# Decode attention with gate and feed-forward: all output weights behind the last values, in runs of eight heads

## The chip, the cores and the metric

The kernel runs on one core of a Trainium2 chip. The core has five engines with instruction queues of their own: TensorE (PE, matrix products), VectorE (DVE), ScalarE (ACT), GpSimd (POOL) and SyncE (SP, which here only issues transfers). Sixteen DMA engines move data between HBM and the on-chip memory (SBUF). Engines wait for each other and for transfers on semaphores. The metric is the time of one execution on the device, in microseconds (us); lower is better. All data is float32.

## The reference

Two batch items, one new position each. The attention block has 32 heads of 128, with a cache of 4096 keys and values per head; the feed-forward block has 1728 hidden units. The result mixes both by a gate:

```python
g = sigmoid((x * gate_w).sum(-1, keepdims=True))          # x: (2, 1, 640)
q = (x @ wq).reshape(B, 1, 32, 128).transpose(0, 2, 1, 3)  # wq: (640, 4096)
p = softmax(einsum("bhqd,bhkd->bhqk", q, k_cache) * 128 ** -0.5)
o = einsum("bhqk,bhkd->bhqd", p, v_cache)                  # caches: (2, 32, 4096, 128)
a = o.transpose(0, 2, 1, 3).reshape(B, 1, 4096) @ wo       # wo: (4096, 640)
b = silu(x @ w1) @ w2                                      # w1: (640, 1728), w2: (1728, 640)
return g * a + (1 - g) * b
```

The caches are 134 MB each, the weights 10.5 MB (wq), 10.5 MB (wo) and 4.4 MB each (w1, w2).

## The kernel before

**Items.** Four heads of one batch item are an item: 16 items, each with 8.4 MB of keys and 8.4 MB of values. SBUF has three large buffers ("slabs") of 8.4 MB, a, b and v. Keys of even items go to b, of odd items to a; values go to v, but those of the last item (15) go to b, in three pieces. The layout is `p c`: partition p holds 128 positions of one head.

**One item.** `query(i)` spreads the item's queries over the partitions (TensorE). `products(i)` multiplies keys with the query in place: GpSimd 60 of the 128 positions of a partition, VectorE 68 (L617). `scores(i)` sums over the head dimension (VectorE, L627), `peak(i)` takes the maximum, `weights(i)` the exponential (ScalarE), which writes the tile `pz`. In the next turn `total`, `values` (32 products of width 512 on TensorE, L707, twice that in records of the profile), `invert`, `combine` (scale and pick out, VectorE), `gather` (TensorE) and `turn` finish the item. `turn` sums the four heads' columns into `row`, transposes it by 32 x 32 blocks and writes the item's columns of `oP`, a tile for each group of four heads with columns for both batch items (0 and 16).

**The order.** Each engine runs its operations in the order in which `f.op` and `f.dma` record them; `Flow.plan` derives the waits from what each reads and writes. All large transfers are issued by SP, in order; an issue waits until the buffer's readers are done, and everything recorded behind it on SP waits with it. In the loop over items SP gets values(i), then keys(i + 2). On TensorE, items 0 to 13 run as loops (one before and one after the middle), where waits are counted down on the semaphores `next_q`, `weights`, `values` and `rows`; the rest is straight code.

**Weights.** SP starts with wq into a and v, w1 into v and keys 0 into b; keys 1 follow when the first part of the query projection has freed a. x and the gate vector are issued by ScalarE. Around item 5 (`MID`), slab a takes the output weights of groups 0 and 1 and w2 in place of keys 7: `project(0)`, `project(1)` and `ffn_out` run there, then keys 7 are loaded. The output weights of groups 2 to 7 go into v after the values of item 14, as six transfers of 1280 KB, the last one cut in 960 and 320 KB.

**The end.** `project(grp)` multiplies a group's four columns with its weights. Groups 0 to 5 are "early": their sums go to two strips of a PSUM bank, width 320. Groups 6 and 7 are "late": four strips, width 160. After the first column of the late ones `merge` copies the early sums (ScalarE, L548) and joins them in (TensorE, L553). VectorE copies the result (L844), SP stores it, and when it has landed GpSimd clears the semaphores (L850).

Of the kernel before, what the change touches and what calls it, by code (L numbers as in the profile page):

```python
# [4 lines left out]
AF = mybir.ActivationFunctionType  # L5
# [137 lines left out]
def gated_decode(nc, x, kc, vc, wq, wo, w1, w2, gate, out):  # L143
    P = 128
# [39 lines left out]
    def part(n, *ks):  # L184
        return [f"{n}.{k}" for k in (ks or range(8))]
# [18 lines left out]
    he = sb("he", [P, FR, B])  # L204
    seq = sb("seq", [P, 2 * FR, B])
    join = sb("join", [P, 2, HB + 1])
    qall = sb("qall", [P, HQ, B, DH])
    qsb = sb("qsb", [P, DH])
    Ss = [sb(f"s{i}", [P, C]) for i in range(2)]
# [1 line left out]
    rs = sb("rs", [P, 1])  # L211
    rg = sb("rg", [P, 1])
    osb = sb("osb", [P, 4, DH])
    turned = sb("turned", [P, 512])
    spaced = sb("spaced", [P, FR, 32])
    row = sb("row", [P, DH])
    oP = [sb(f"oP{i}", [P, Q, 32]) for i in range(HQ)]
    oT = sb("oT", [P, Q, 32])
    partial = sb("partial", [P, W2])
    ot = sb("ot", [P, W])  # L220

# [8 lines left out]
    W1_AT = (J - J0) * H * DH  # L230
    XG_AT = W1_AT + J * F
    HD = D // 2
    WO_MID = 2
    WO_AT = {}
    for grp in range(HQ):
        WO_AT[grp] = FH * HD + grp * QD * D // P if grp < WO_MID else (grp - WO_MID) * QD * D // P
# [17 lines left out]
    def load_v(i):  # L254
        src = run_of(vflat, i)
        if i < N - 1:
            v_load[i] = f.dma("SP", slab["v"], src, writes=part("v"), signal=h_v if i < LOOPED else None)
            return
        cuts = (0, SLAB // 2, 3 * SLAB // 4, SLAB)
        after = f.users(part("b"))  # L260
        for k, (c0, c1) in enumerate(zip(cuts, cuts[1:])):
            f.dma("SP", slab["b"][:, c0:c1], src[:, c0:c1], writes=part("b", k), after=after)

    def load_wo(grp, n, key, after):
        at = WO_AT[grp]
        src = wo[grp * QD : (grp + 1) * QD, :].rearrange("(p n) d -> p (n d)", n=Q)
        cuts = (0, Q * D - D, Q * D) if grp == HQ - 1 else (0, Q * D)
        for k, (c0, c1) in enumerate(zip(cuts, cuts[1:])):
            f.dma("SP", slab[n][:, at + c0 : at + c1], src[:, c0:c1], writes=part(n, key + k), after=after)
# [6 lines left out]
    f.dma("ACT", xg[:B], x.rearrange("b s d -> (b s) d"), writes=part("v", 6))  # L276
    f.dma("ACT", xg[B : B + 1], gate[None, :], writes=part("v", 7))
    f.dma("SP", slab["v"][:, :W1_AT], wq_rows[:, SLAB:], writes=part("v", 0))
    f.dma(
        "SP",  # L280
# [14 lines left out]
    )  # L295
    f.op("POOL", lambda: G_.memset(xz, 0.0), writes=["xz"])
    f.op("POOL", lambda: G_.memset(pz, 0.0), writes=["pz"])
    f.op("POOL", lambda: G_.memset(partial, 0.0), writes=["partial", "partial2", "partial3"])
# [22 lines left out]
    f.op("DVE", lambda: V.memset(pick, 0.0), writes=["pick"])  # L321
    f.op(
        "DVE",
        lambda: V.reduce_sum(pick[:, 0:P:32], sel.rearrange("p (q c) -> p q c", c=4), axis=AX.X),
        reads=["sel"],
        writes=["pick"],
    )
# [2 lines left out]
        lambda: V.reduce_sum(own, sel.rearrange("p (q c) -> p c q", c=4), axis=AX.X),  # L330
        reads=["sel"],
        writes=["own"],
    )
    for q in range(Q):
        f.op(
# [177 lines left out]
    for e in range(2):  # L513
# [51 lines left out]
    def project(grp, n, key):  # L565
        w = slab[n][:, WO_AT[grp] : WO_AT[grp] + Q * D]
        to = "early" if grp < LAST else "late"
        for k in range(Q):
            lhsT = oP[grp][:, k, :] if count[to] == 0 else oP[grp][:, k, : HB + 1]
            wk = part(n, key + (grp == HQ - 1 and k == Q - 1))  # L570
            accumulate(lhsT, w[:, k * D : (k + 1) * D], [f"oP{grp}", f"oP{grp}b"], wk, to)
            if count["late"] == 1:
                merge()

    def ffn_out(n):

        def fn():  # L580
            for k in range(FH):
                to = 64 + 32 * (k % 2)
                last = T_.matmul(  # L583
                    early[to : to + 2 * B, :],
                    seq[:, k : k + 2, :].rearrange("p k b -> p (k b)"),
                    slab[n][:, k * HD : (k + 1) * HD],
                    start=(k < 2),
                    stop=(k >= FH - 2),
                )
            return last  # L590

        f.op("PE", fn, reads=["seq0", "seq1"] + part(n, 2), writes=["ps_acc"])
# [106 lines left out]
        )  # L699

    def values(i, by=(), loop=None):
        v = slab["v" if i < N - 1 else "b"].rearrange("p (g c) -> p g c", g=NG)

        def groups(g0, g1):
            for gr in range(g0, g1):
# [22 lines left out]
        for k, (g0, g1) in enumerate(zip(cuts, cuts[1:])):  # L728
            f.op(
                "PE",  # L730
                lambda g0=g0, g1=g1: groups(g0, g1),
                reads=part("b", k) + ["pz"],
                writes=["ps_v"],
            )

# [25 lines left out]
        )  # L761

    def turn(i):
        hq, b = items[i]
        f.op(
            "DVE",
            lambda: V.reduce_sum(row, ps_o.rearrange("p (c d) -> p d c", d=DH), axis=AX.X),  # L767
            reads=["ps_o"],
            writes=["row"],
        )  # L770
        dst, key = (oP[hq], f"oP{hq}") if b == 0 else (oT, "oT")
        f.op(
            "DVE",
            lambda: V.transpose(dst, row.rearrange("p (i n) -> p n i", n=Q)),
            reads=["row"],
            writes=[key],
        )
        if b == 1:
            f.op(
                "DVE",  # L780
                lambda: V.tensor_copy(oP[hq][:, :, HB : HB + 1], oT[:, :, 0:1]),
                reads=["oT", f"oP{hq}"],
                writes=[f"oP{hq}b"],
            )

    for i in range(N + 1):
# [12 lines left out]
        if i < N and i != MID:  # L801
            load_v(i)
        if i < N:
            scores(i)
            if 1 <= i <= LOOPED:
                relay(i)
            if i + 2 < N and i != MID:
                load_k(i + 2)
            peak(i)
            weights(i)  # L810
        if i == MID:
            after = f.users(part("a"))
            for grp in range(WO_MID):
                load_wo(grp, "a", grp, after)
            f.dma(
                "SP",
                slab["a"][:, : FH * HD],
                w2.rearrange("(p r) (e c) -> p (r e c)", p=P // 2, e=2).rearrange("p (e c) -> (p e) c", e=2),
                writes=part("a", 2),
                after=after,  # L820
            )
            load_v(i)
        if i == N - 1:
            after = f.users(part("v"))
            for grp in range(WO_MID, HQ):
                load_wo(grp, "v", grp - WO_MID, after)
# [4 lines left out]
        if i == 0:  # L831
            query(1)
        elif i + 1 < N:
            query(i + 1, by=by("relay"), loop=loop)
# [7 lines left out]
    for grp in range(WO_MID, HQ):  # L842
        project(grp, "v", grp - WO_MID)
    f.op("DVE", lambda: V.tensor_copy(ot, acc), reads=["ps_acc"], writes=["ot"])  # L844
    left = f.dma("SP", out.rearrange("b s (n d) -> (s n) b d", n=G), ot[0:P:HB, :], reads=["ot"])

    def clear():
        ids = sorted(s.num for s in f.sems)
        assert ids == list(range(ids[0], ids[-1] + 1))
        return G_.sem_clear(range(ids[0], ids[-1] + 1))  # L850

    f.op("POOL", clear, after=[left])

# [36 lines left out]
```

## Time and profile before

| | before |
|---|---|
| median of 3 runs | 697.12 us (696.89 to 698.07) |
| profiled execution | 697.13 us |
| its span | 695.1 us |
| HBM read | 298.26 MB, 429 GB/s over the span |
| busiest engine | VectorE, 479.2 us (69%) |
| TensorE | 223.0 us (32%) |

The span runs from the first to the last instruction; the execution's own time has 2.0 us more around it. PE is TensorE's products, PEld its weight loads, SPq and ACTq the issuing of transfers by SyncE and ScalarE. A float32 product stands in the profile as two records. In a timeline row the first number is the start, the second the length, and the bracket at the end the idle time before it and what ended it. The chain lists, in order of time, the work that each later step had to wait for, back from the last instruction.

### The profile page before, as it was taken

To read this page: it belongs to the slowest core of one execution; us is meant where nothing else is said; L and a number is where in the kernel's file an instruction comes from. 1 tells how busy PE (TensorE), PEld (TensorE's weight loads), DVE (VectorE), ACT (ScalarE), POOL (GpSimd) and SP (SyncE) were. 2 spreads that over 40 slices of the span, in tenths; PEclk is the share of its full clock that TensorE was granted. 3 is DMA by queue.
4 is the path that set the end of the run, shared out by engine and by line. 5 is a ranking of instruction groups with operands and counts; after the bars stand their busy time and mean duration, and the time that the engine had idled before them with its cause. 6 is when DMAs were issued, how large, how long until landed. Compare 5 with 4: busy or idle time off the path is not lost. (4 is left out here: it accounts for less than half of the span.)

```text
span 695.1 us, 3615 instructions
## 1 busy us (share of the span) xinstructions
PE 223.0 (32%) x1478; PEld 73.7 (11%) x1478; DVE 479.2 (69%) x236; ACT 40.8 (6%) x154; POOL 265.0 (38%) x25
## 2 busy tenths in 40 slices
PE   1630043240605053542140606041240605050376
PEld 1110011010201011110010202010010101010022
DVE  2016998969688695195949688694949588695930
ACT  0010001010101001001010101001010101001010
POOL 1006291808080624502609081533518080624400
PEclk9985556565757567877575757566575757566599
DMA  9999999999999999999999999999999999999997
GB/s 419 406 453 422 426 422 456 442 426 426 422 449 449 426 426 420 454 430 431 422 437 449 430 434 422 437 449 427 434 426 430 453 430 426 434 426 456 407 422 312
DMA packets 6794, 298.38 MB, mean 429 GB/s; under 512 B 759, under 2 KB 767, under 8 KB 1026
## 3 DMA queue, kind: packets, MB, share of 16 engines
q1 hardware_dynamic: 6780, 298.26, 99.3%
q8 instruction: 5, 0.08, 0.0%
q14 instruction: 3, 0.02, 0.0%
q10 hardware_dynamic: 6, 0.01, 0.0%
HBM read 298.26 MB, written 0.01 MB: 429 GB/s over the span
## 5 line engine op out<-in xcount | busy, mean ns | idle before, releaser
L707 PE MATMUL ps<-slab_v,pz 128*32 128x512 f32 x960 | 138.9, 743 | 352.9 <-PEq L129 326.8
L611 POOL TENSOR_TENSOR slab_b<-slab_b,qsb 128x7680 f32<-128x7680 f32 x8 | 131.4, 16428 | 203.9 <-DMA slab_b<-in_A_k_cache_dram 189.0
L611 POOL TENSOR_TENSOR slab_a<-slab_a,qsb 128x7680 f32<-128x7680 f32 x8 | 131.5, 16439 | 181.9 <-DMA slab_a<-in_A_k_cache_dram 168.5
L627 DVE TENSOR_REDUCE s<-slab_b 128x68 f32<-128x8704 f32 (+1 forms) x16 | 138.2, 8677 | 0.0
L627 DVE TENSOR_REDUCE s<-slab_a 128x68 f32<-128x8704 f32 (+1 forms) x16 | 138.1, 8676 | 0.0
L617 DVE TENSOR_TENSOR slab_b<-slab_b,ps 128x8704 f32<-128x8704 f32 x8 | 73.7, 9216 | 54.1 <-DMA slab_b<-in_A_k_cache_dram 54.1
L617 DVE TENSOR_TENSOR slab_a<-slab_a,ps 128x8704 f32<-128x8704 f32 x8 | 73.8, 9222 | 45.2 <-DMA slab_a<-in_A_k_cache_dram 42.8
L707 PEld LDWEIGHTS ps<-slab_v,pz 128*32 128x32 f32 x960 | 37.9, 133 | 441.5 <-issue 415.3
L656 ACT ACTIVATE pz<-s,nb 32x128 f32<-32x128 f32 x64 | 25.5, 398 | 547.4 <-PE ps L707 413.7
L755 PE MATMUL ps<-osb,pick 128*128 128x512 f32 x32 | 19.5, 694 | 26.8 <-PEq L129 24.9
L767 DVE TENSOR_REDUCE row<-ps 128x128 f32<-128x512 f32 x16 | 11.1, 692 | 22.3 <-PE ps L755 22.3
L739 DVE SCALAR_TENSOR_TENSOR osb<-ps,rg,own 128x512 f32<-128x512 f32 x16 | 12.0, 750 | 18.7 <-PE ps L707 18.7
L499 DVE COPY spaced<-ps 128x224 f32<-128x224 f32 x2 | 0.7, 387 | 27.8 <-PE ps L481 27.8
L432 PE MATMUL ps<-qall,spread 128*128 (+1 forms) x32 | 7.2, 310 | 25.4 <-DVE slab_b L617 24.7
L693 DVE RECIPROCAL ps<-ps 128x1 f32<-128x1 f32 x16 | 2.7, 169 | 16.9 <-PE ps L681 16.9
L535 PE MATMUL ps<-slab_v,oP 128*17 128x320 f32 (+2 forms) x128 | 11.9, 367 | 2.3 <-DMA slab_v<-in_A_wo_dram 2.2
L681 PE MATMUL ps<-rs,fold 128*128 128x1 f32 x32 | 6.1, 259 | 19.9 <-PEq L129 19.7
L412 PE MATMUL ps<-slab_a,xz 128*32 128x512 f32 x64 | 9.5, 758 | 8.6 <-DMA slab_a<-in_A_wq_dram 8.6
L656 ACT ACTIVATION_READ_ACCUMULATOR pz<-s,nb 32x1 f32 x64 | 11.8, 184 | 0.0
L583 PE MATMUL ps<-slab_a,seq 128*4 128x320 f32 x54 | 9.3, 501 | 7.5 <-DMA slab_a<-in_B_w_dram 7.5
L432 PEld LDWEIGHTS ps<-qall,spread 128*128 128x128 f32 x32 | 6.7, 216 | 34.9 <-DVE slab_b L617 25.5
L844 DVE COPY ot<-ps 128x160 f32<-128x160 f32 x1 | 0.3, 325 | 13.6 <-PE ps L535 13.6
(68 smaller groups left out, 97.4 us busy)
## 6 DMA issues: line engine op xcount, KB each, us to landing
slab_v<-in_A_wo_dram SPq DMA_DIRECT2D x5, 1280.0 KB, 18.2
slab_v<-in_B_w_dram SPq DMA_DIRECT2D x1, 4320.0 KB, 37.2
slab_a<-in_B_w_dram SPq DMA_DIRECT2D x1, 4320.0 KB, 27.5
slab_b<-in_A_v_cache_dram SPq DMA_DIRECT2D x1, 4096.0 KB, 37.9
slab_b<-in_A_v_cache_dram SPq DMA_DIRECT2D x2, 2048.0 KB, 44.5
slab_a<-in_A_wo_dram SPq DMA_DIRECT2D x2, 1280.0 KB, 16.2
slab_v<-in_A_wq_dram SPq DMA_DIRECT2D x1, 2048.0 KB, 26.3
slab_v<-in_A_wo_dram SPq DMA_DIRECT2D x1, 960.0 KB, 25.2
```

The lines of the kernel that those rows point to most:

```text
L412: last = T_.matmul(qr[u][32 * q : 32 * q + 32, :], xz[:, j, :], w[:, u * HALF : (u + 1) * HALF, q, :], start=(j == 0), stop=(j == J - 1),)
L432: return T_.matmul(ps_q[:, :DH], spread, qall.rearrange("p h b d -> p (h b) d")[:, i, :], start=True, stop=True,)
L535: last = T_.matmul(dst[32 * n : 32 * n + m, :], lhsT, w[:, n * width : (n + 1) * width], start=first, stop=final,)
L583: last = T_.matmul(early[to : to + 2 * B, :], seq[:, k : k + 2, :].rearrange("p k b -> p (k b)"), slab[n][:, k * HD : (k + 1) * HD], start ...
L611: lambda: G_.tensor_mul(k[:, CV:, :], k[:, CV:, :], qsb[:, None, :].to_broadcast([P, C - CV, DH])),
L617: lambda: V.tensor_mul(k[:, :CV, :], k[:, :CV, :], ps_q[:, None, :DH].to_broadcast([P, CV, DH])),
L627: lambda c0=c0, c1=c1: V.reduce_sum(Ss[i % 2][:, c0:c1], k[:, c0:c1, :], axis=AX.X),
L656: last = S_.activation(pz[lo:hi, :, 4 * q : 4 * q + 4], s[lo:hi].rearrange("p (g c) -> p g c", c=4), AF.Exp, bias=nb[lo:hi], scale=SCALE, ...
L707: last = T_.matmul(ps_v[32 * q : 32 * q + 32, :], pz[:, gr, :], v[:, gr, :], start=(gr < 4), stop=(gr >= NG - 4),)
L739: lambda: V.scalar_tensor_tensor(osb, ps_v.rearrange("p (c d) -> p c d", d=DH), rg, own[:, :, None].to_broadcast([P, 4, DH]), op0=ALU.mult ...
L755: lambda *_: T_.matmul(ps_o, pick, osb.rearrange("p c d -> p (c d)"), start=True, stop=True),
L767: lambda: V.reduce_sum(row, ps_o.rearrange("p (c d) -> p d c", d=DH), axis=AX.X),
```

## The change

- Output weights: none in the middle any more. All eight groups are loaded after the last values, in four runs of eight heads (2.6 MB each): runs 0 to 2 into v, run 3 into b in three pieces (1280, 960 and 320 KB). Runs 0 to 2 are early, run 3 is late. Each run is projected with eight columns.
- w2 is loaded in front, into b, ahead of the first keys, and `ffn_out` runs there. Keys of even items now go to a, of odd items to b; the first keys are issued where keys 1 were, values 0 after the first feed-forward product, keys 1 after `ffn_out`. The last values go to a.
- TensorE runs items 0 to 14 in one loop, with the query of the next item at its head.
- `turn` puts two groups into one tile: it sums on 64 partitions, copies the row twice side by side, transposes eight blocks instead of four and adds the two halves with masks (`side`), five or six VectorE operations instead of two or three.
- Ends: a first exponential on ScalarE, and the table load with it, stands ahead of the issues of x and the gate vector. The semaphores are cleared once SP has issued the output, and GpSimd waits for its landing after that; `s_out` and `s_sent` are counted down by their waits.

```diff
-    LAST = HQ - 2
+    NP = HQ // 2
+    PR = 2 * Q
...
-    MID = 5
-    LOOPED = N - 2
+    LOOPED = N - 1
+    s_out, s_sent = nc.alloc_semaphore("output"), nc.alloc_semaphore("sent")
...
     def kslab(i):
-        return "b" if i % 2 == 0 else "a"
+        return "a" if i % 2 == 0 else "b"
...
+    def load_wo(g):
+        n, at = ("v", g * PD) if g < NP - 1 else ("b", 0)
+        src = wo[g * PR * P : (g + 1) * PR * P, :].rearrange("(p n) d -> p (n d)", n=PR)
+        cuts = (0, PD) if g < NP - 1 else (0, PD // 2, PD - D, PD)
+        after = f.users(part(n)) if g in (0, NP - 1) else wo_after
         for k, (c0, c1) in enumerate(zip(cuts, cuts[1:])):
+            f.dma("SP", slab[n][:, at + c0 : at + c1], src[:, c0:c1], writes=part(n, g % (NP - 1) + k), after=after)
+        return after
...
-    load_k(0)
+    f.dma(
+        "SP",
+        slab["b"][:, : FH * HD],
+        w2.rearrange("(p r) (e c) -> p (r e c)", p=P // 2, e=2).rearrange("p (e c) -> (p e) c", e=2),
+        writes=part("b"),
+    )
...
+    f.op("ACT", lambda: S_.activation(ge, ones[:, :B], AF.Exp, scale=-1.0), reads=["ones"], writes=["ge"])
+    f.dma("ACT", xg[:B], x.rearrange("b s d -> (b s) d"), writes=part("v", 6))
+    f.dma("ACT", xg[B : B + 1], gate[None, :], writes=part("v", 7))
...
     f.op("PE", lambda: mm_qr(0, J0), reads=part("a") + ["xz"], writes=["ps_0", "ps_1"])
-    load_k(1)
+    load_k(0)
...
+    load_v(0)
...
-    total_of = {"early": Q * LAST, "late": Q * (HQ - LAST) + 1}
+    total_of = {"early": PR * (NP - 1), "late": PR + 1}
...
+    def project(g):
+        n, at = ("v", g * PD) if g < NP - 1 else ("b", 0)
+        w = slab[n][:, at : at + PD]
+        to = "early" if g < NP - 1 else "late"
+        for k in range(PR):
+            lhsT = oP[g][:, k, :] if count[to] == 0 else oP[g][:, k, : HB + 1]
+            key = g if g < NP - 1 else (k >= PR // 2) + (k == PR - 1)
+            accumulate(lhsT, w[:, k * D : (k + 1) * D], [f"oP{g}{u}{b}" for u in range(2) for b in range(B)], part(n, key), to)
             if count["late"] == 1:
                 merge()
...
+    ffn_out("b")
+    load_k(1)
...
     def turn(i):
         hq, b = items[i]
+        gr, u = divmod(hq, 2)
...
+        for e in range(2):
+            f.op("DVE", lambda e=e: V.tensor_copy(row2[:, :, 16 * e : 16 * e + 16], row.rearrange("p (i n) -> p n i", n=PR)), ...)
+        f.op("DVE", lambda: V.transpose(oT, row2), ...)
+        f.op("DVE", lambda: V.tensor_scalar(oE, oT[:, :, 0], side[:64, 0:1], None, op0=ALU.mult), ...)
+        f.op("DVE", lambda: V.scalar_tensor_tensor(oP[gr][64 * u : 64 * u + 64, :, HB * b], oT[:, :, 1], side[:64, 1:2], oE, op0=ALU.mult, op1=ALU.add), ...)
...
-            if 1 <= i <= LOOPED:
+            if i < LOOPED:
                 relay(i)
...
-        if i == MID:
-            after = f.users(part("a"))
-            for grp in range(WO_MID):
-                load_wo(grp, "a", grp, after)
-            f.dma("SP", slab["a"][:, : FH * HD], w2..., writes=part("a", 2), after=after)
-            load_v(i)
         if i == N - 1:
+            wo_after = None
+            for g_ in range(NP):
+                wo_after = load_wo(g_)
...
         if i + 1 < N:
+            query(i + 1, by=[ops["relay", i]], loop=i)
             copy_q(i + 1)
-        if i == MID:
-            for grp in range(WO_MID):
-                project(grp, "a", grp)
-            ffn_out("a")
-            load_k(i + 2)
+    for g_ in range(NP):
+        project(g_)
...
+    f.dma("SP", out.rearrange("b s (n d) -> (s n) b d", n=G), ot[0:P:HB, :], reads=["ot"], signal=s_out)
+    sent = f.op("SP", lambda: nc.sync.sem_inc(s_sent), after=[])
+    sent.signal = "sent"
     def clear():
         ids = sorted(s.num for s in f.sems)
+        G_.wait_ge(s_sent, 1).then_inc(s_sent, -1)
+        G_.sem_clear(range(ids[0], ids[-1] + 1))
+        return G_.wait_ge(s_out, 16).then_inc(s_out, -16)
```

More of the change, by code (lines that the diff above doesn't have):

```diff
@@ L206, in gated_decode @@
     join = sb("join", [P, 2, HB + 1])
+    turned = sb("turned", [P, FR * 32])
+    spaced = sb("spaced", [P, FR, 32])
+    oT, row2 = turned[:64, : PR * 32].rearrange("p (n r) -> p n r", r=32), spaced[:64, :PR, :]
     qall = sb("qall", [P, HQ, B, DH])
@@ L213, in gated_decode @@
     osb = sb("osb", [P, 4, DH])
[L214 to L218, printed above, removed]
+    row = sb("row", [64, DH])
+    oP = [sb(f"oP{i}", [P, PR, 32]) for i in range(NP)]
+    oE = sb("oE", [64, PR])
+    side = sb("side", [P, 2])
     partial = sb("partial", [P, W2])
@@ L232, in gated_decode @@
     HD = D // 2
[L233 to L236, printed above, removed]
+    PD = PR * D
     def kslab(i):
-        return "b" if i % 2 == 0 else "a"
+        return "a" if i % 2 == 0 else "b"
     kflat = kc.rearrange("b (g q) s d -> b g (q s d)", q=Q)
@@ L323, in gated_decode @@
         "DVE",
-        lambda: V.reduce_sum(pick[:, 0:P:32], sel.rearrange("p (q c) -> p q c", c=4), axis=AX.X),
+        lambda: V.reduce_sum(
+            pick.rearrange("p (a b) -> p a b", b=32)[:, : Q // 2, :2],
+            sel.rearrange("p (a b c) -> p a b c", b=2, c=4),
+            axis=AX.X,
+        ),
         reads=["sel"],
@@ L332, in gated_decode @@
         writes=["own"],
+    )
+    f.op(
+        "DVE",
+        lambda: V.reduce_sum(side, ident.rearrange("p (a e i) -> p e a i", e=2, i=16), axis=AX.XY),
+        reads=["ident"],
+        writes=["side"],
     )
@@ L563, in merge @@
         count["late"] += 1
[L565 to L571, printed above, removed]
+    def project(g):
[6 more added lines that the diff above has]
+            accumulate(lhsT, w[:, k * D : (k + 1) * D], [f"oP{g}{u}{b}" for u in range(2) for b in range(B)], part(n, key), to)
             if count["late"] == 1:
@@ L590, in fn @@
             return last
-        f.op("PE", fn, reads=["seq0", "seq1"] + part(n, 2), writes=["ps_acc"])
+        f.op("PE", fn, reads=["seq0", "seq1"] + part(n), writes=["ps_acc"])
         for k in range(2):
@@ L731, in values @@
                 lambda g0=g0, g1=g1: groups(g0, g1),
-                reads=part("b", k) + ["pz"],
+                reads=part("a", k) + ["pz"],
                 writes=["ps_v"],
@@ L764, in turn @@
         hq, b = items[i]
+        gr, u = divmod(hq, 2)
         f.op(
             "DVE",
-            lambda: V.reduce_sum(row, ps_o.rearrange("p (c d) -> p d c", d=DH), axis=AX.X),
+            lambda: V.reduce_sum(row, ps_o[:64].rearrange("p (c d) -> p d c", d=DH), axis=AX.X),
             reads=["ps_o"],
@@ L770, in turn @@
         )
-        dst, key = (oP[hq], f"oP{hq}") if b == 0 else (oT, "oT")
+        for e in range(2):
+            f.op(
+                "DVE",
+                lambda e=e: V.tensor_copy(row2[:, :, 16 * e : 16 * e + 16], row.rearrange("p (i n) -> p n i", n=PR)),
+                reads=["row"],
+                writes=[f"spaced{e}"],
+            )
+        f.op("DVE", lambda: V.transpose(oT, row2), reads=["spaced0", "spaced1"], writes=["turned"])
         f.op(
             "DVE",
-            lambda: V.transpose(dst, row.rearrange("p (i n) -> p n i", n=Q)),
-            reads=["row"],
-            writes=[key],
-        )
[L778 to L784, printed above, removed]
+            lambda: V.tensor_scalar(oE, oT[:, :, 0], side[:64, 0:1], None, op0=ALU.mult),
+            reads=["turned", "side"],
+            writes=["oE"],
+        )
+        f.op(
+            "DVE",
+            lambda: V.scalar_tensor_tensor(
+                oP[gr][64 * u : 64 * u + 64, :, HB * b],
+                oT[:, :, 1],
+                side[:64, 1:2],
+                oE,
+                op0=ALU.mult,
+                op1=ALU.add,
+            ),
+            reads=["turned", "oE", "side", f"oP{gr}"],
+            writes=[f"oP{gr}{u}{b}"],
+        )
     for i in range(N + 1):
@@ L800, in gated_decode @@
             invert(j)
-        if i < N and i != MID:
+        if 1 <= i < N:
             load_v(i)
@@ L804, in gated_decode @@
             scores(i)
-            if 1 <= i <= LOOPED:
+            if i < LOOPED:
                 relay(i)
-            if i + 2 < N and i != MID:
+            if i + 2 < N:
                 load_k(i + 2)
@@ L830, in gated_decode @@
             turn(j)
[L831 to L834, printed above, removed]
         if i + 1 < N:
+            query(i + 1, by=[ops["relay", i]], loop=i)
             copy_q(i + 1)
-        if i == MID:
-            for grp in range(WO_MID):
-                project(grp, "a", grp)
-            ffn_out("a")
-            load_k(i + 2)
-    for grp in range(WO_MID, HQ):
-        project(grp, "v", grp - WO_MID)
+    for g_ in range(NP):
+        project(g_)
     f.op("DVE", lambda: V.tensor_copy(ot, acc), reads=["ps_acc"], writes=["ot"])
-    left = f.dma("SP", out.rearrange("b s (n d) -> (s n) b d", n=G), ot[0:P:HB, :], reads=["ot"])
+    f.dma("SP", out.rearrange("b s (n d) -> (s n) b d", n=G), ot[0:P:HB, :], reads=["ot"], signal=s_out)
+    sent = f.op("SP", lambda: nc.sync.sem_inc(s_sent), after=[])
+    sent.signal = "sent"
     def clear():
@@ L849, in clear @@
         assert ids == list(range(ids[0], ids[-1] + 1))
-        return G_.sem_clear(range(ids[0], ids[-1] + 1))
-    f.op("POOL", clear, after=[left])
+        G_.wait_ge(s_sent, 1).then_inc(s_sent, -1)
+        G_.sem_clear(range(ids[0], ids[-1] + 1))
+        return G_.wait_ge(s_out, 16).then_inc(s_out, -16)
+    f.op("POOL", clear)
     f.plan()
```

24 lines of the change are left out of this document (4 added, 20 removed).

## The prediction

> **What bounds the kernel now.** I read the page's totals first, then the DMA share by stretches, then the chain that ended last, then the timeline where the chain passes. The page:
>
> ```profile
> span 695.1 us, 3615 instructions
> ...
> PE 223.0 (32%) x1478; PEld 73.7 (11%) x1478; DVE 479.2 (69%) x236; ACT 40.8 (6%) x154; POOL 265.0 (38%) x25
> ...
> DMA  9999999999999999999999999999999999999997
> ...
> q1 hardware_dynamic: 6780, 298.26, 99.3%
> q8 instruction: 5, 0.08, 0.0%
> ```
>
> No engine is busy for more than 69% of the span, while the transfers fill every slice but the last. The windows say how full:
>
> ```profile
> core 0: us, PE busy (x) PEld busy (x) DVE busy (x) ACT busy (x) POOL busy (x), PEclk, DMA share, GB/s
> ...
> 21.70:651.70 630.00, 188.69 (x1196) 60.94 (x1196) 459.95 (x194) 36.93 (x143) 262.93 (x16) 0.64 1.00 434
> ...
> 690.00:691.00 1.00, 0.93 (x28) 0.82 (x32) 0.00 (x0) 0.01 (x1) 0.00 (x0) 1.00 0.43 172
> 691.00:692.00 1.00, 0.92 (x30) 0.60 (x25) 0.00 (x0) 0.00 (x0) 0.00 (x0) 1.00 0.14 56
> ```
>
> For 630 us the DMA share is 1.00, at 434 GB/s. The change moves the same 298.26 MB, so the middle can neither gain nor lose unless the queue runs dry. What is left to win or lose is the head (before the first byte), the tail (after the last) and the evenness with which the 16 engines finish. The chain shows the tail, the timeline how TensorE keeps up with the output weights (L535):
>
> ```profile
> 665.62 23.39 DMA slab_v<-in_A_wo_dram
> ...
> 689.05 0.52 PE ps L535 x8
> 689.57 0.02 issue
> 689.60 0.43 ACT partial L548
> 690.02 0.04 issue
> 690.07 0.47 PE ps L553 x8
> 690.53 0.81 PE ps L535 x24
> 691.35 0.08 issue
> 691.43 1.32 PE ps L535 x32
> ...
> 692.77 0.33 DVE ot L844
> ```
>
> ```profile
> 673.78 1.92 PE L707 MATMUL ps<-slab_b,pz 128*32 128x512 f32 x16 [2.17 <-DMA slab_b<-in_A_v_cache_dram]
> 676.65 1.12 PE L755 MATMUL ps<-osb,pick 128*128 128x512 f32 x2 [0.94 <-DVE osb L739]
> 677.71 4.50 PE L535 MATMUL ps<-slab_v,oP 128*17 128x320 f32 x32
> 682.96 2.33 PE L535 MATMUL ps<-slab_v,oP 128*17 128x320 f32 x16 [0.75 <-DMA slab_v<-in_A_wo_dram]
> 686.00 2.34 PE L535 MATMUL ps<-slab_v,oP 128*17 128x320 f32 x16 [0.71 <-DMA slab_v<-in_A_wo_dram]
> ```
>
> A group of four heads is one transfer and 16 matmul records of width 320. Groups land at 682.96, 686.00 and 689.05, so 3.05 us apart, and cost 2.34 us each: TensorE waits for each, and the last two groups, in the cheaper width 160, run behind the last bytes and end at 692.75.
>
> **The change, part by part.**
>
> *Does the queue run dry in the middle?* The steady state of an item:
>
> ```profile
> 615.84 9.87 PE L707 MATMUL ps<-slab_v,pz 128*32 128x512 f32 x64 [27.29 <-PEq L129]
> ...
> 625.77 0.33 SPq L68 DMA_DIRECT2D slab_v<-in_A_v_cache_dram  x1
> ...
> 628.53 0.40 DVE L774 STREAM_TRANSPOSE oT<-row 128x128 f32<-128x128 f32 x1
> 628.97 0.17 DVE L781 COPY oP<-oT 128x4 f32<-128x4 f32 x1
> 635.14 9.22 DVE L617 TENSOR_TENSOR slab_a<-slab_a,ps 128x8704 f32<-128x8704 f32 x1 [5.99 <-DMA slab_a<-in_A_k_cache_dram]
> ```
>
> The next values are issued at 625.77, when the value product (L707) has freed their buffer. The keys ahead of them land at 635.14. So 9.4 us of queued transfer are left at the tightest point. The new order keeps this: the same loads wait for the same readers, only the two key buffers swap names, and one TensorE loop runs the same sequence (query, total, values, gather) that two loops and loose code ran. Cost nothing, hidden by those 9.4 us. The longer `turn` replaces a transpose of 128 columns and, every second item, a small copy by two copies of 128 columns, a transpose of 256 and two small operations. At 0.40 for the transpose and 0.17 for a small operation, with twice those for the larger ones as an upper bound, that is 0.7 to 1.5 us more of VectorE per item. It comes right before the 5.99 us in which VectorE waits for keys, and is hidden there.
>
> *The head.* Rows of the start:
>
> ```profile
> 0.73 0.54 ACTq L68 DMA_DIRECT2D slab_v<-in_A_x_dram  x1
> 0.74 0.39 SPq L68 DMA_DIRECT2D slab_a<-in_A_wq_dram  x1
> 1.57 1.28 ACT L391 ACT_TABLE_LOAD   x1 [1.57 <-PEq L882]
> 10.35 2.36 PE L365 MATMUL ps<-ident,slab_v 3*128 3x3 f32 x10 [10.35 <-DMA slab_v<-in_gate_w_dram]
> 12.82 0.17 DVE L376 COPY xz<-ps 128x10 f32<-128x10 f32 x1 [9.07 <-PE ps L365]
> 22.72 9.47 PE L412 MATMUL ps<-slab_a,xz 128*32 128x512 f32 x64 [8.62 <-DMA slab_a<-in_A_wq_dram]
> 38.84 3.83 PE L481 MATMUL ps<-slab_v,xz 128*32 128x432 f32 x40 [2.02 <-DMA slab_v<-in_B_w_dram]
> ```
>
> The table load and a first exponential now stand ahead of ScalarE's two small issues, about 1.5 us later for x. Its product is ready at 12.99 and needed at 22.72: 9.7 us of cover. Without that cover it would cost those 1.5 us. The large issue on SP stays at 0.74. It could gain if the neighbouring ScalarE issue holds it up: at most 0.54, at least 0. I take 0, because SP's issue starts 0.01 us after the other and is no longer than it.
>
> *The second feed-forward matrix moved to the front.* At 434 GB/s its 4.4 MB take 10.2 us, 8.39 MB of keys or values 19.3 us. First matrix landed at 38.84, second at 49.0, keys 0 (issued after L412, near 32) at 68.3, values 0 (issued near 42.7) at 87.7. Keys 1 are now queued on SP behind its product:
>
> ```profile
> L627 DVE TENSOR_REDUCE s<-slab_b 128x68 f32<-128x8704 f32 (+1 forms) x16 | 138.2, 8677 | 0.0
> ...
> L583 PE MATMUL ps<-slab_a,seq 128*4 128x320 f32 x54 | 9.3, 501 | 7.5 <-DMA slab_a<-in_B_w_dram 7.5
> ```
>
> That product took 9.3 us; even twice as long (half clock) it frees its buffer at 67.6, while the queue holds until 87.7: 20 us of cover, and what waits behind keys 1 on SP (keys 2, values 1) needs VectorE first. Keys 2 wait for the scores of item 0: 68.3 + 9.2 (L617) + 2 x 8.7 (L627) = 94.9, and the queue then holds until 87.7 + 19.3 = 107.0. Values 1 wait for the value product of item 0, about 108, when keys 2 last to 126. Cost nothing; in the middle the matrix and two groups no longer interrupt, which gains nothing either, as the bytes remain.
>
> *The output weights in four runs.* This is where I see a cost. A run of eight heads is 2.6 MB, 2 x 3.05 = 6.1 us apart, and 32 early records. The row at 677.71 is just such a piece: 4.50 us. All four run after the last values. Those land just before 673.78 now (L707's last piece waits for them), so after the change about 6.1 earlier; the runs land near 673.8, 679.9 and 686.0, the first half of the fourth at 689.05 as now. TensorE waits for the first two. But after 686.00 it has 4.50 us of work instead of 2.34, and reaches the fourth run at 690.3 to 690.5 instead of 689.05. From there the chain is that of now: 8 records, ScalarE copy, join at +1.02, so at 691.3 to 691.5 instead of 690.07; then the 2.68 us to 692.75, less the up to 0.27 us by which the records from 691.43 wait for the next piece (690.53 + 0.81 = 691.34 for the 24, which are modelled ends). The end of L535 moves from 692.75 to between 693.7 and 694.2: +1.0 to +1.45. A bound below is 0, if records run faster than these. I take +1.0, as records of the two widths follow without a gap when data are there (690.07 + 0.47 = 690.54, and the next at 690.53).
>
> *Transfers of the weights.* 3.045 us per 1280 KB is 430 GB/s against 434 in the long stretch: 0.03 us per group. Eight heads make the pieces per partition twice as long. I take half of that back for six groups, -0.1, with bounds -0.2 and 0. That a transfer of its own costs next to nothing in the queue is read from the same 3.05 us; the small output shows what one costs that runs alone:
>
> ```profile
> 693.13 0.68 SPq L68 DMA_DIRECT2D out_dram<-ot  x1
> ```
>
> It is issued at 693.13 and the last instruction starts at 694.9 (below): 1.8 us for 5 KB. Six transfers replace nine, so if each carried this cost, 5.4 us would go; that is a rival.
> The Trainium skill's page "DMA: Bandwidth & Descriptors", section "Anatomy of one DMA — SWDGE (gpsimd) path", puts such a fixed part at about 2 us for a DMA issued from GpSimd, most of it the receipt of the write; by it the sum would be 6 us lower. The trace disagrees for transfers queued back to back on SP: 1280 KB take 3.05 us in all.
>
> *The end.*
>
> ```profile
> L850 POOLq EVENT_SEMAPHORE_RANGE_CLEAR  x1: 269/269/269, 694.9 to 694.9; - x1
> ```
>
> It starts at 694.9 after the output has landed, and the span ends at 695.1. Cleared while the output is under way (about 2 us from the end of L844 to there), only a short wait remains: -0.25, bounds -0.27 and 0.
>
> *Evenness of the 16 engines.* After 690.0 the engines have 0.43 + 0.14 = 0.57 us each left on average, but the last one works into the slice that ends at 692. Even engines would end up to 1.4 us earlier. One cause I suspect are the five instruction blocks on q8: 16 KB each, 0.6 us on one engine at 434/16 GB/s. TensorE's program loses one copy of the loop body and one of the value product, so one or two blocks fewer. Which engine a block takes, the profile doesn't show. I take 0, bounds -1.4 and +0.7 (one more block on the engine that is last).
>
> **Sum**: +1.0 - 0.1 - 0.25 + 0 + 0 = +0.65 us. The profiled execution took 697.13 for its span of 695.1, and the median of the runs is 697.12, so they stand level: 697.8 us. About 0.2%, or 1.4 us, is what a measurement of this kernel can tell from no change, so I call this no change.
>
> **The rivals.**
> 1. *The wider runs don't delay the tail.* If the fourth run's chain starts with its landing after all, only the trims remain: -0.35, 696.8. Against it stands the 4.50 us row. Still no change.
> 2. *Slower: an instruction block falls on the engine that ends last.* The third run then lands 0.6 us later, two of them 1.2, and the tail adds to it: +1.25 to +1.85, 698.4 to 699.0. It decides once the last engine lags 0.75 us more than now. For it: the lag exists (the 0.14 row) and the order of all blocks changes. Against it: fewer blocks.
> 3. *Faster: the engines end evenly, or the head gains.* -1.2 of lag and -0.5 of head, with the tail cost: -1.05, 696.1; without the tail cost -2.05, 695.1. Two of these three have to come together for more than 0.2%.
> 4. *Faster: each transfer has a cost of its own in the queue, and three fewer save 3 x 1.8 = 5.4 us*: 692.4. The 3.05 us between groups speaks against it. [...]
> 5. *The queue runs dry at the front*: values 1 or keys 2 late by more than the 12 us of cover; say 5 us beyond it, 702.8. Nothing in the rows speaks for it.
>
> **How the numbers follow.** Forecast 0.59, rival 1 0.17: both within 0.2%, and 0.01 of rival 2 too, so same 0.77. Rival 3 0.07 and rival 4 0.01: faster 0.08. Rival 2 beyond 698.5 0.13 and rival 5 0.02: slower 0.15. The range reaches to rival 3's first case and rival 2's upper end: 696.2 to 699.0; the likeliest case's own range is 697.1 to 698.4.
>
> **What would show it.** In the changed profile: DMA share 1.00 at 434 GB/s in the long stretch; SP's first issue still near 0.74; x's product before 22; the three early runs on L535's successor of about 4.5 us each, the third starting near 686 and the width-160 records only near 690.3; the merge copy near 690.8; the output copy near 693.8; no clear at the end. Wrong it would be by a slice of lower DMA share before 650, by runs that start with their landing at the end, or by a last landing that has moved by more than a microsecond.

## The result, and the profile after

The changed kernel takes 856.67 us (median of 5; 856.35 to 857.24), the kernel before 697.23 us in the same comparison: 1.2286 times as long, 95% interval 1.2272 to 1.23. I had forecast no change, 697.8 us, with a range to 699.0. The whole of this case is about the 159 us that I didn't see.

The page of the changed kernel, parts 1, 2, 3 and 5:

```profile
span 855.0 us, 3688 instructions
...
PE 219.5 (26%) x1478; PEld 75.4 (9%) x1478; DVE 719.5 (84%) x293; ACT 41.0 (5%) x155; POOL 267.7 (31%) x29
...
DMA  9999999999696895969599695959779594968930
...
q1 hardware_dynamic: 6348, 298.26, 81.8%
...
L805 DVE COPY spaced<-row 64x128 f32<-64x128 f32 x32 | 235.1, 7384 | 0.6
L640 POOL TENSOR_TENSOR slab_a<-slab_a,qsb 128x7680 f32<-128x7680 f32 x8 | 132.3, 16534 | 275.3 <-ACT qsb L477 210.2
```

The bytes are the same 298.26 MB, but the transfers fill 81.8% of the span instead of 99.3%: from the eleventh slice on the queue runs dry once in each item. VectorE went from 479.2 to 719.5 us, and 235.1 us of that are one line, the two copies in `turn` (L805), at 7384 ns in the mean for 128 elements per partition. And GpSimd's product (L640) now waits mostly for the new query (qsb). In the kernel before it waited for keys:

```profile
L611 POOL TENSOR_TENSOR slab_b<-slab_b,qsb 128x7680 f32<-128x7680 f32 x8 | 131.4, 16428 | 203.9 <-DMA slab_b<-in_A_k_cache_dram 189.0
```

Keys are no longer what is late.

A mean over two kinds hides what happens. The timeline of the changed kernel, where it first goes wrong (the turn of item 0, while item 2 begins):

```profile
138.20 0.68 DVE L798 TENSOR_REDUCE row<-ps 64x128 f32<-64x512 f32 x1 [2.23 <-PE ps L784]
...
138.62 0.27 ACT L477 COPY qsb<-ps 128x128 f32<-128x128 f32 x1 [1.28 <-PE ps L455]
138.91 16.75 DVE L805 COPY spaced<-row 64x128 f32<-64x128 f32 x2
138.96 16.57 POOL L640 TENSOR_TENSOR slab_a<-slab_a,qsb 128x7680 f32<-128x7680 f32 x1 [14.98 <-ACT qsb L477]
...
156.57 9.21 DVE L646 TENSOR_TENSOR slab_a<-slab_a,ps 128x8704 f32<-128x8704 f32 x1
```

The pair of copies and GpSimd's product start and end together. In the trace the first copy starts 0.05 us ahead of the product and takes 0.27 us. The second starts 0.14 us behind it, takes 16.56 us and ends 0.13 us after the product's end at 155.53. It looks as if the copy isn't slow but held, which e1 below settles. The profile counts the hold as busy time of VectorE, not as a wait, which is why the list of waits shows nothing of it. This happens in 14 of the 16 turns, always to the second copy. The two turns at the end, with no product left, take 0.45 us for both copies.

What this does to an item, from GpSimd's own timeline and two windows that each hold one item:

```profile
237.04 16.54 POOL L640 TENSOR_TENSOR slab_a<-slab_a,qsb 128x7680 f32<-128x7680 f32 x1 [32.48 <-ACT qsb L477]
286.17 16.53 POOL L640 TENSOR_TENSOR slab_b<-slab_b,qsb 128x7680 f32<-128x7680 f32 x1 [32.58 <-ACT qsb L477]
335.29 16.56 POOL L640 TENSOR_TENSOR slab_a<-slab_a,qsb 128x7680 f32<-128x7680 f32 x1 [32.59 <-ACT qsb L477]
```

```profile
232.00:281.00 49.00, 10.81 (x70) 3.64 (x70) 46.44 (x17) 2.23 (x9) 16.54 (x1) 0.60 0.81 342
281.00:330.00 49.00, 10.14 (x70) 3.53 (x70) 46.45 (x17) 2.22 (x9) 16.53 (x1) 0.60 0.80 343
```

An item takes 49.1 us, of which VectorE is busy for 46.4, the hold included; the transfers of an item need 38.6 and have a share of 0.8. VectorE is the bound.

### The profile page after: what moved, and what is told of

Its sections match the earlier page's. It is cut to its first block, busy times and chain, and to the rows that moved or that the text cites. A ratio compares the mean times of both kernels' runs of the same rounds, so it can differ in the third digit from the quotient of the medians.

```text
span 855.0 us, 3688 instructions
## 1 busy us (share of the span) xinstructions
PE 219.5 (26%) x1478; PEld 75.4 (9%) x1478; DVE 719.5 (84%) x293; ACT 41.0 (5%) x155; POOL 267.7 (31%) x29
## 3 DMA queue, kind: packets, MB, share of 16 engines
q1 hardware_dynamic: 6348, 298.26, 81.8%
HBM read 298.26 MB, written 0.01 MB: 349 GB/s over the span
## 5 line engine op out<-in xcount | busy, mean ns | idle before, releaser
L805 DVE COPY spaced<-row 64x128 f32<-64x128 f32 x32 | 235.1, 7384 | 0.6
L640 POOL TENSOR_TENSOR slab_a<-slab_a,qsb 128x7680 f32<-128x7680 f32 x8 | 132.3, 16534 | 275.3 <-ACT qsb L477 210.2
L640 POOL TENSOR_TENSOR slab_b<-slab_b,qsb 128x7680 f32<-128x7680 f32 x8 | 132.3, 16535 | 249.8 <-ACT qsb L477 227.7
L784 PE MATMUL ps<-osb,pick 128*128 128x512 f32 x32 | 31.8, 1096 | 557.9 <-PEq L129 557.0
L736 PE MATMUL ps<-slab_v,pz 128*32 128x512 f32 x960 | 122.9, 670 | 7.4 <-PEq L129 7.4
L784 PEld LDWEIGHTS ps<-osb,pick 128*128 128x128 f32 x32 | 7.8, 303 | 572.0 <-issue 570.2
L798 DVE TENSOR_REDUCE row<-ps 64x128 f32<-64x512 f32 x16 | 10.9, 682 | 34.7 <-PE ps L784 34.7
L736 PEld LDWEIGHTS ps<-slab_v,pz 128*32 128x32 f32 x960 | 30.9, 122 | 86.1 <-issue 85.8
L455 PE MATMUL ps<-qall,spread 128*128 (+1 forms) x32 | 10.2, 420 | 36.6 <-PEq L129 35.9
L455 PEld LDWEIGHTS ps<-qall,spread 128*128 128x128 f32 x32 | 10.2, 326 | 52.5 <-issue 50.9
L560 PE MATMUL ps<-slab_v,oP 128*17 128x320 f32 (+1 forms) x96 | 13.1, 433 | 0.0
L868 DVE COPY ot<-ps 128x160 f32<-128x160 f32 x1 | 0.3, 324 | 14.1 <-PE ps L560 14.1
L609 PE MATMUL ps<-slab_b,seq 128*4 128x320 f32 x54 | 10.2, 540 | 6.4 <-DMA slab_b<-in_B_w_dram 6.4
```

The source lines that it names most:

```text
L455: return T_.matmul(ps_q[:, :DH], spread, qall.rearrange("p h b d -> p (h b) d")[:, i, :], start=True, stop=True,)
L560: last = T_.matmul(dst[32 * n : 32 * n + m, :], lhsT, w[:, n * width : (n + 1) * width], start=first, stop=final,)
L609: last = T_.matmul(early[to : to + 2 * B, :], seq[:, k : k + 2, :].rearrange("p k b -> p (k b)"), slab[n][:, k * HD : (k + 1) * HD], start ...
L640: lambda: G_.tensor_mul(k[:, CV:, :], k[:, CV:, :], qsb[:, None, :].to_broadcast([P, C - CV, DH])),
L736: last = T_.matmul(ps_v[32 * q : 32 * q + 32, :], pz[:, gr, :], v[:, gr, :], start=(gr < 4), stop=(gr >= NG - 4),)
L784: lambda *_: T_.matmul(ps_o, pick, osb.rearrange("p c d -> p (c d)"), start=True, stop=True),
```

## The experiments

Theory P: VectorE's copy in `turn` and GpSimd's product exclude each other; whichever starts second is held until the other ends. Rival C: the strided copy on 64 partitions is slow by its own form. Rival O: the new order (second matrix in front, query at the loop's head) makes VectorE late.

**e1: let the product start after turn.** Each operation stays, only GpSimd's start is moved.

```diff
             reads=["qsb"] + k1,
             writes=k1,
+            after=[ops["turn", i - 2]] if i >= 2 else (),
...
-        f.op(
+        ops["turn", i] = f.op(
```

> The changed kernel; GpSimd's key product additionally waits for the last VectorE operation of the turn recorded before it. No operation is taken away. Theory P (in the changed kernel the second copy of turn starts 0.14 us after GpSimd's product and ends 0.13 us after it, 16.5 us instead of 0.27: the copy and the product exclude each other): all 32 copies take 0.3 us, VectorE's busy time falls from 720 to about 490 us, and the time is what was forecast for the rest of the change, 696.9 to 698.5 us. Rival C (a copy of 64 partitions with a stride of 8 elements is slow by its own form): the copies stay at 7.4 us in the mean, time about 855. Rival O (the new order, with the second feed-forward matrix ahead of the keys and the query at the loop's head, makes VectorE late): copies 0.3 us, but keys still wait for scores, DMA share below 0.9, time over 750.

Measured: 698.21 us against 697.38 before, ratio 1.001 (1.0001 to 1.0019). Its page:

```profile
span 696.0 us, 3688 instructions
...
PE 224.4 (32%) x1478; PEld 74.7 (11%) x1478; DVE 493.3 (71%) x293; ACT 41.0 (6%) x155; POOL 266.2 (38%) x29
...
q1 hardware_dynamic: 6348, 298.26, 99.1%
```

And its group of the copies (from the list of all groups):

```profile
L806 DVE COPY spaced<-row 64x128 f32<-64x128 f32 x32 | 7.2, 263 | 0.6
```

The same 32 copies, 263 ns each, and the whole loss is gone. Rival C falls (same form, in the mean 28 times faster), and so does rival O (the new order is untouched, and the DMA share is back).

**e2, e3, e8: which operations are held.** If the conflict is over a way into SBUF, then where an operand lies should decide. e2 puts `row` and the transposed tile `oT` into PSUM, e3 only `row`, e8 is e2 with a second transposed copy in SBUF as an input of the last operation.

```diff
-    row = sb("row", [64, DH])
+    row = ps_m[:64, 128 : 128 + DH]                               # e2, e3, e8
+    oT = ps_m[:64, 256:512].rearrange("p (n r) -> p n r", r=32)   # e2, e8
...
+        f.op("DVE", lambda: V.transpose(oS, row2), ..., writes=["turned2"])   # e8: oS in SBUF
...
-                oT[:, :, 1],
+                oS[:, :, 1],                                      # e8
```

> The changed kernel; the tiles row and oT lie in PSUM instead of SBUF, so that none of turn's VectorE operations reads and writes SBUF with two streams: the copies go from PSUM to SBUF, the transpose from SBUF to PSUM, the last operation has one input in each. GpSimd's product may start whenever it likes. Theory P in its narrow form (it is a second SBUF stream of VectorE that GpSimd's product excludes): nothing is blocked although the product starts in the middle of turn, copies about 0.3 us, time 697 to 699. Rival P-wide (any copy of VectorE is blocked while GpSimd works): time stays near 855. Rival O: over 750.

> The changed kernel; only row lies in PSUM, so the copies have one SBUF side, but the multiply by a mask from oT to oE and the masked sum after it still work from SBUF to SBUF. Theory P-narrow: the copies are free (0.3 us), and the wait moves to one of the two operations behind the transpose, up to 16.5 us each item; time again 840 to 860. If those small operations (8 elements per partition) don't need the second stream, time 697 to 699: then only the copies did it.

> As e2, but the masked sum (L819 there) takes its first input from a second copy of the transposed tile in SBUF, so that it has two inputs in SBUF, as in the changed kernel; one VectorE transpose of 0.45 us more in each item. Theory P, wide for inputs: it is blocked until GpSimd's product ends, about 15 us in each item, time 840 to 850. Theory P, narrow (only operations with one input and one output in SBUF take the second stream): no wait, 698 to 699 us.

Measured: e2 698.11 us (ratio 1.001, 1.0 to 1.0019); e3 843.93 (1.21, 1.2078 to 1.2122); e8 839.86 (1.2041, 1.2019 to 1.2063), which is 0.14 below the lower end that theory P in its wide form gave. In e2 the product starts in the middle of turn as in the changed kernel, and nothing is held. VectorE's timeline of e2, then GpSimd's:

```profile
138.74 0.48 DVE L806 COPY spaced<-ps 64x128 f32<-64x128 f32 x2
139.25 0.45 DVE L810 STREAM_TRANSPOSE ps<-spaced 64x256 f32<-64x256 f32 x1
139.74 0.22 DVE L813 TENSOR_SCALAR oE<-ps,side 64x8 f32<-64x8 f32 x1
139.99 0.22 DVE L819 SCALAR_TENSOR_TENSOR oP<-ps,side,oE 64x8 f32<-64x8 f32 x1
```

```profile
138.78 16.58 POOL L641 TENSOR_TENSOR slab_a<-slab_a,qsb 128x7680 f32<-128x7680 f32 x1 [14.97 <-ACT qsb L478]
```

In e3 the copies are free and the hold moves on to the mask multiply, eight elements per partition (VectorE's timeline of e3, then GpSimd's):

```profile
138.86 0.48 DVE L805 COPY spaced<-ps 64x128 f32<-64x128 f32 x2
139.37 0.44 DVE L809 STREAM_TRANSPOSE turned<-spaced 64x256 f32<-64x256 f32 x1
139.84 15.53 DVE L812 TENSOR_SCALAR oE<-turned,side 64x8 f32<-64x8 f32 x1
```

```profile
138.90 16.45 POOL L640 TENSOR_TENSOR slab_a<-slab_a,qsb 128x7680 f32<-128x7680 f32 x1 [14.99 <-ACT qsb L477]
```

In e8 it moves to the sum with two inputs in SBUF, while a transpose from SBUF to SBUF beside it runs freely (timeline of e8):

```profile
138.84 16.53 POOL L641 TENSOR_TENSOR slab_a<-slab_a,qsb 128x7680 f32<-128x7680 f32 x1 [14.99 <-ACT qsb L478]
...
139.68 0.40 DVE L811 STREAM_TRANSPOSE turned<-spaced 64x256 f32<-64x256 f32 x1
140.01 0.17 DVE L814 TENSOR_SCALAR oE<-ps,side 64x8 f32<-64x8 f32 x1
140.22 15.18 DVE L820 SCALAR_TENSOR_TENSOR oP<-turned,side,oE 64x8 f32<-64x8 f32 x1
```

So three of turn's operations are held when their operands lie in SBUF: the copy, the multiply by a mask, and the sum of two inputs. The changed kernel shows it for the copy only because that one comes first. In all three the hold ends 0.02 to 0.13 us behind GpSimd's product. The transpose isn't held, though it reads and writes SBUF (0.44 us in e3, 0.40 in e8); why it differs, the runs don't show. Nor is VectorE's own product held, which takes its second input from PSUM: in the kernel before (L617) it takes 9.18 us where it starts 0.29 us into GpSimd's product.

The Trainium skill's page "SBUF — State Buffer", section "Who interferes with whom", states this rule: VectorE has one pair of SBUF ports of its own and shares a second with GpSimd. By that section, copies and `tensor_scalar` may run in modes that use both pairs, an operation with two SBUF inputs reads its second one through the shared pair when GpSimd reads SBUF too, and whoever comes first keeps the pair for its whole instruction while the other fully blocks. The trace agrees where GpSimd comes first: the held instructions take 16.56, 15.53 and 15.18 us. No run here shows the other direction, GpSimd held by VectorE, clearly.

**e6: a shorter product.** `CV = 98` instead of 68 gives GpSimd 30 of 128 positions instead of 60.

> The changed kernel; CV 98 instead of 68, so GpSimd multiplies 30 of 128 positions instead of 60, VectorE 98. Theory P: the blocked copy lasts as long as the product, 8.3 instead of 16.5 us; VectorE's product lasts 13.3 instead of 9.2 us. An item falls from 49.1 by 8.25 and rises by 4.1, to 44.9 us; over the 14 locked items -59 us, so about 797 us. If the copies were slow for another reason they would stay at 16.5 us and VectorE's larger share would make it slower, about 914 us.

Measured: 803.23 us (1.1515, 1.1494 to 1.1537), near the 797. GpSimd's timeline of e6:

```profile
187.76 8.48 POOL L640 TENSOR_TENSOR slab_b<-slab_b,qsb 128x3840 f32<-128x3840 f32 x1 [36.48 <-ACT qsb L477]
232.72 8.46 POOL L640 TENSOR_TENSOR slab_a<-slab_a,qsb 128x3840 f32<-128x3840 f32 x1 [36.48 <-ACT qsb L477]
```

The item takes 45.0 us, as expected (44.9). The copies' group fell from 7384 to 3846 ns in the mean: the hold has the length of the product. Of the 6 us that I missed, 3.9 lie ahead of the first held turn, whose product starts at 142.86 instead of 138.96. The rest is small: an item saves 4.1 us, from 49.1 to 45.0, where I had 4.2.

**e4: the copies alone, in the kernel before.** Two copies of `row` into the tile `spaced`, which nothing reads then.

```diff
+        for e in range(2):
+            f.op("DVE", lambda e=e: V.tensor_copy(spaced[:64, : 2 * Q, 16 * e : 16 * e + 16], row[:64]...), reads=["row"], writes=[f"spaced{e}"])
```

> The kernel before; turn gets the two copies of the change (row to the tile spaced, which nothing reads then), nothing else. Theory P: the copies alone do it, also in the old order. Item 2's keys are there early in both kernels, so its product starts within turn and blocks the second copy for 16.4 us. Each locked item takes about 48.5 us instead of 38.6. The middle (output weights and second matrix in place of keys 7) makes keys 7 late and may end it: 740 to 755 if it does, 830 to 850 if not. Rival C: copies slow everywhere, about 850. Rival O: no change, 697 to 699.

Measured: 739.35 us (1.0601, 1.0581 to 1.062). GpSimd's timeline of e4:

```profile
119.77 16.50 POOL L611 TENSOR_TENSOR slab_b<-slab_b,qsb 128x7680 f32<-128x7680 f32 x1 [14.89 <-ACT qsb L454]
168.06 16.57 POOL L611 TENSOR_TENSOR slab_a<-slab_a,qsb 128x7680 f32<-128x7680 f32 x1 [31.79 <-ACT qsb L454]
...
313.63 16.54 POOL L611 TENSOR_TENSOR slab_b<-slab_b,qsb 128x7680 f32<-128x7680 f32 x1 [32.04 <-ACT qsb L454]
367.73 16.43 POOL L611 TENSOR_TENSOR slab_a<-slab_a,qsb 128x7680 f32<-128x7680 f32 x1 [37.56 <-DMA slab_a<-in_A_k_cache_dram]
406.35 16.43 POOL L611 TENSOR_TENSOR slab_b<-slab_b,qsb 128x7680 f32<-128x7680 f32 x1 [22.19 <-DMA slab_b<-in_A_k_cache_dram]
```

The time lies just below the 740 that I had as the lower end. Items 2 to 6 are held, 48 us each. Then the weights in the middle make keys 7 late; the product starts at 367.73, 6 us after turn, and from there no copy is held again, at 38.6 us an item. So the two copies alone suffice, in the old order too. And there are two regimes. While VectorE is late, keys are already there, GpSimd starts the moment the new query is written, that is, in the middle of turn, and this keeps VectorE late. Once keys are the last to come, turn is over long before, and the two never meet.

**e5: protect only items 2 to 7.** The wait of e1, with `if 2 <= i <= 7`.

> The changed kernel; GpSimd's product waits for the turn recorded before it for items 2 to 7 alone, items 8 to 15 are as in the changed kernel. Theory P with memory (two regimes: while VectorE is late, GpSimd starts on the new query, in the middle of turn, which keeps VectorE late; once VectorE has caught up, GpSimd starts when keys land, some 6 us after turn, and the two never meet): no copy over 0.3 us in any item, time as with all items protected, 697.6 to 698.6 us. Rival (the copies and the product meet at every unprotected item): items 8 to 15 take 49 us instead of 38.6 each, copies of 16.5 us, time 770 to 790.

Measured: 698.15 us (1.001, 1.0 to 1.0019), and no copy over 271 ns in any item. GpSimd's timeline of e5:

```profile
140.43 16.59 POOL L640 TENSOR_TENSOR slab_a<-slab_a,qsb 128x7680 f32<-128x7680 f32 x1 [16.45 <-DVE oP L819]
173.18 16.48 POOL L640 TENSOR_TENSOR slab_b<-slab_b,qsb 128x7680 f32<-128x7680 f32 x1 [16.16 <-DVE oP L819]
205.93 16.43 POOL L640 TENSOR_TENSOR slab_a<-slab_a,qsb 128x7680 f32<-128x7680 f32 x1 [16.27 <-DVE oP L819]
242.73 16.43 POOL L640 TENSOR_TENSOR slab_b<-slab_b,qsb 128x7680 f32<-128x7680 f32 x1 [20.37 <-DMA slab_b<-in_A_k_cache_dram]
...
397.25 16.42 POOL L640 TENSOR_TENSOR slab_b<-slab_b,qsb 128x7680 f32<-128x7680 f32 x1 [22.16 <-DMA slab_b<-in_A_k_cache_dram]
```

Only items 2, 3 and 4 use the protection; from item 5 on keys come last. Eight unprotected items run freely. The loss of 159 us hangs on three starts in the first 210 us; whether fewer would do was not tried. These three starts are 32.75 us apart: that is VectorE's pace while it is late and nothing is held. With 16.3 us of hold on top (16.55 instead of 0.27) it makes the 49.1 us of the changed kernel, and the 38.6 us of the transfers leave it 5.9 us of slack, far less than a hold.

**e7: the tail.** e2, with the third run of output weights loaded as two transfers, so that TensorE needn't wait for all of it.

```diff
-        cuts = (0, PD) if g < NP - 1 else (0, PD // 2, PD - D, PD)
+        cuts = (0, PD) if g < NP - 2 else (0, PD // 2, PD) if g == NP - 2 else (0, PD // 2, PD - D, PD)
```

> Row and oT in PSUM as in e2, and the third run of output weights is loaded in two transfers of 1280 KB, so that TensorE starts on its first half 3 us earlier. Theory T (the tail of the changed kernel is 1.0 us longer because TensorE gets its last early run in one piece, at 686, with 4.5 us of work): the join starts near 690.1 instead of 691.2 or later, the output copy near 692.7 instead of 693.65, and the time falls by 0.9 to 1.1 us against e2, to 697.0 to 697.4, within 0.05% of the kernel before. Rival (something else of the change costs the 0.7 us, such as a later end of the transfers): time as e2.

Measured: 697.27 us against 697.41 before (0.9997, 0.9988 to 1.0006), 0.84 less than e2 (0.87 when each is set against the kernel before of its own series), a little under the 0.9 to 1.1 that I expected. Below, the end of the chain of e1, then that of e7:

```profile
686.10 4.82 PE ps L560 x32
...
691.42 0.47 PE ps L578 x8
691.88 1.95 PE ps L560 x56
...
693.85 0.32 DVE ot L869
```

```profile
689.23 0.51 PE ps L561 x8
...
690.24 0.47 PE ps L579 x8
690.71 2.06 PE ps L561 x56
...
692.79 0.33 DVE ot L869
```

With the cut the late part starts with its landing, and the output copy is back at 692.79 (693.65 in e2). This is the best version of the change. It doesn't beat the kernel before by anything that can be measured.

## Why the prediction was wrong, point by point

**The step that failed: "0.7 to 1.5 us more of VectorE per item ... hidden there".** It is two mistakes in one. The size: I priced the new operations by rows of the trace in which GpSimd was idle (0.17 and 0.40 us). Without a hold that price is right: in e1 VectorE is busy for 14.1 us more than before, 0.88 an item. Beside a running product, the second copy costs what is left of the product, 16.56 us. The cover: I read 5.99 us of idle time ahead of VectorE's next product in one late item and took it for all. In the first turn there is none (2.95 us in the second), and the trace of before had the rows. VectorE's timeline of before, in the turn of item 0, then GpSimd's:

```profile
118.76 0.69 DVE L767 TENSOR_REDUCE row<-ps 128x128 f32<-128x512 f32 x1 [2.23 <-PE ps L755]
119.49 0.41 DVE L774 STREAM_TRANSPOSE oP<-row 128x128 f32<-128x128 f32 x1
119.82 9.18 DVE L617 TENSOR_TENSOR slab_b<-slab_b,ps 128x8704 f32<-128x8704 f32 x1
```

```profile
119.53 16.44 POOL L611 TENSOR_TENSOR slab_b<-slab_b,qsb 128x7680 f32<-128x7680 f32 x1 [14.89 <-ACT qsb L454]
```

The product starts 0.04 us into the transpose, and VectorE goes on without a gap. A transpose isn't held, so this cost nothing before; the one small copy of the old turn (L781) came only in turns of odd items, about 3 us or more ahead of the product. I asked of each added operation how long it takes and whether VectorE had room, not what else is running at that moment and whether the two can run together. None of my rivals was of that kind, though the Trainium skill's page "SBUF — State Buffer" has the rule.

**"The new order keeps this"**, the 9.4 us of queued transfer in the steady state, failed with it: in the changed kernel that steady state is never reached. The sign that I had named for being wrong, a lower DMA share before 650, did come, but rival 5 had the queue run dry once, at the front, by 5 us; it runs dry in every item from 222 us on. An engine's slack of 6 us an item, once overdrawn by a step of 16, became a different steady state.

**The rest came out near the forecast**, as e1, e2 and e5 show, which are the change without the hold: +0.83, +0.73 and +0.74 us against the kernel before, where I had +0.65.
- Tail, +1.0 forecast: the third run starts at 686.10, the join at 691.42 (forecast 691.3 to 691.5), the output copy at 693.85 instead of 692.77, so +1.08 (+0.88 in e2); e7 takes it away. Right.
- End, -0.25 forecast: from the output copy's start to the end of the span 2.15 us in e1 (696.0 - 693.85) and 2.1 in e7, against 2.3 before (695.1 - 692.77). Right, within the rounding.
- Larger pieces, -0.1 forecast: can't be told. TensorE starts on the third run at 686.10 in e1 and at 685.90 in e2, and the kernel before had as much of the weights at 686.00.
- Head and front, 0 forecast: SP's first issue stays at 0.74, x's product starts at 12.76 instead of 10.35 in the changed kernel, 2.4 us later where I had 1.5, and delays nothing, and keys 1, keys 2 and values 1 were issued at 59.91, 95.41 and 107.95 (forecast: at the latest 67.6, then 94.9 and 108). Right.
- The engines' unevenness, 0 forecast: the slices after 690 have shares of 0.36 and 0.15 in e1, against 0.43 and 0.14. As expected, q8 carries one instruction block fewer (four instead of five), but q14 one more (four instead of three). That such blocks cause the unevenness was not tried and stays open.

## What to carry to other kernels

Before pricing an operation that is added to VectorE, list what GpSimd does at that moment, in the earliest and tightest item as well as in the steady state: beside a GpSimd product of two SBUF operands, the only kind tried here, a copy or a multiply by a per-partition scalar from SBUF to SBUF, or an operation with two SBUF inputs, cost what was left of GpSimd's instruction. Cures are to put operands in PSUM or to let GpSimd start after the small operations; both gave back the 159 us but for the 0.7 to 0.8 us of the longer tail. And when an operation's mean looks absurd, compare its start and end with the other engines' instructions before blaming its shape.

## What the runs showed of the hardware that I had not expected

- A VectorE instruction of eight elements per partition took 15.53 us beside a GpSimd product, and the profile books that as busy time. GpSimd's product took 16.57 us where it began within a copy of 0.27 us, against 16.43 in most items; but it also took 16.59 us once in e5, where no copy ran beside it, so these rows show no hold of GpSimd by VectorE.
- A transpose from SBUF to SBUF was not held (0.40 us in e8 in the same place where the next operation was held for 15.18).
- Whether turns are held at the start decides the regime of all later items: 49.1 us each in the changed kernel, 38.6 in e5, with the same instructions and waits from item 8 on.
